# A cached attention block on one core: the last weight row as two partial loads, and rounds with branch hints moved

## The chip, the core and the metric

The kernel runs on one core of a Trainium2 chip, all in float32. The metric is the time of one execution in microseconds (us) on the device. A profiled execution gives the trace: when each instruction of TensorE (PE, with its weight loads as PEld), VectorE (DVE), ScalarE (ACT), GpSimd (POOL) and SyncE (SP) ran, and what the 16 DMA engines moved.

## The reference

One decoding step of two sequences: attention over a cache of 4096 positions with 32 heads of 128, beside a small feed-forward network, mixed by a gate.

```python
def reference(A_x, A_k_cache, A_v_cache, A_wq, A_wo, B_x, B_w1, B_w2, gate_w):
    x = A_x                                                  # (2, 1, 640)
    g = _sigmoid((x * gate_w).sum(-1, keepdims=True))
    q = (x @ wq).reshape(B, Sq, H, Dh) ...                   # B = 2, Sq = 1, H = 32, Dh = 128
    scores = jnp.einsum("bhqd,bhkd->bhqk", q, k_cache) * (Dh ** -0.5)
    p = _softmax(scores, axis=-1)
    o = jnp.einsum("bhqk,bhkd->bhqd", p, v_cache)
    a = o ... reshape(B, Sq, H * Dh) @ wo                    # wo: (4096, 640)
    b = silu(x @ w1) @ w2                                    # F = 1728
    return g * a + (1 - g) * b
```

The two caches hold 2 x 32 x 4096 x 128 floats each, 268 MB together; wq and wo have 10 MB each, w1 and w2 4.4 MB each.

## The kernel before, in words

`gated_decode` writes the whole program through a small recorder, `Flow`. `f.op` and `f.dma` note an operation with what it reads and writes; `f.plan` then works out which earlier operations each has to wait for, and the engine programs are put out one engine at a time. A DMA has a semaphore of its own and is waited for with a constant; `count` gives it a shared one. Line 72 of the profile is the DMA call in `Flow.dma`, lines 131, 153, 156, 172 and 176 are the waits and loop instructions.

Four ways of putting out operations matter here. `run` writes them straight. `repeat` writes one item's operations as a counted loop (PE's loop over the first 15 items). `climb` does so for DVE, two items a turn. `once` writes operations as the body of a loop that runs one time: a register is set to 0, the body begins with a place for a branch hint, and at the end 1 is added and a branch back to the head is tested and not taken.

```python
with nc.body(head, valid_engines=on):
    place = e.mark_branch_hint_location()
    self.run(eng, ops)
    nc.regs_alu(regs, regs, 1, op=ALU.add)
    e.br_lt(regs, 1, on_true=head, on_false=end).branch_hint(place)
```

Before the change one such round exists, on PE, around the last 33 operations (the whole output projection).

The stages. First w1, x, the gate's weights, w2 and wq are loaded (x and the gate's weights in rows of 640 bytes), DVE forms x @ w1 by multiply-adds (lines 474 and 477), PE the feed-forward output (line 569) into `ps_acc` and the queries (line 644). SP also writes zeros to the output at the start. Then come 16 items, an item being four heads of one sequence: its K is a slab of 128 partitions x 64 KiB, 8.39 MB, and so is its V. Three slabs of that size fill most of the on-chip memory: "v" for V, "a" and "b" for K of even and odd items. POOL (line 709) and DVE (line 715) multiply K by the query in place, DVE sums (line 725) and finds the maximum, ACT takes the exponentials (line 754), PE multiplies them by V in 32 groups (line 801), gathers (line 839), and DVE puts the heads' outputs into `oP` (lines 854 to 873). SP issues the K load of item i + 2 as soon as the sums of item i are done with that slab, and the V load of item i as soon as PE is done with V of item i - 1. The V of the last item goes to slab "a".

The output projection. The rows of wo form four groups of PR = 8 row sets; a row set is 128 partitions x 640 floats (2560 bytes a partition). `load_wo` issues, all behind the last V: groups 0 and 1 in one load of 5120 KB, group 2 in two loads of 1280 KB each (all into slab "v"), group 3 into slab "b" in three loads, of FIRST = 5 rows (1600 KB), 2 rows (640 KB) and the last row (320 KB). The keys `v.0` to `v.3` and `b.0` to `b.2` carry who waits for which load. `in_halves(g)` multiplies groups 0 to 2 with the heads in `oP` (line 592): each of 8 steps a group has two matmuls of 320 columns, to two blocks of 32 rows of `ps_acc`. In groups 0 and 1 the steps alternate between the upper and the lower 64 rows (`to = 64 * (s_ % 2)`); in group 2, from `PACED` on, all go to the upper 64. `merge` copies `ps_acc` to SBUF on ACT (line 604) and joins its parts into `ps_0` on PE (line 609). `in_quarters(3)` adds group 3 (line 622): 8 steps of four matmuls of 160 columns, the first five waiting for the first load, two for the second, one for the third. In the trace each matmul has two passes. DVE copies the result (line 930) and SP writes the output.

Of the kernel before, what the change touches and what calls it, by code (L numbers as in the profile page):

```python
# [189 lines left out]
def gated_decode(nc, x, kc, vc, wq, wo, w1, w2, gate, out):  # L190
    P = 128
    B, H, SK, DH = kc.shape
    D = x.shape[2]
# [13 lines left out]
    HB = 16  # L207
    CV = 68
    G = 4
    W = D // G  # L210
    W2 = D // 2
    NP = HQ // 2
    PR = 2 * Q
    FIRST = 5
    LEAD = HB // 2
    PACED = (NP - 2) * PR
    items = [(2 * n + u, b) for n in range(NP) for b in range(B) for u in range(2)]
    N = len(items)
    LOOPED = N - 1
# [2 lines left out]
    f = Flow(nc)  # L222
    V, S_, T_, G_ = nc.vector, nc.scalar, nc.tensor, nc.gpsimd

    def sb(name, shape, align=32):
        return nc.alloc_sbuf_tensor(name, shape, F32, align_bytes=align)[tuple([slice(None)] * len(shape))]

    def bank(name):
        return nc.alloc_psum_tensor(name, [P, 512], F32)[:, :]
# [4 lines left out]
    slab = {n: slabs[:, k * SLAB : (k + 1) * SLAB] for k, n in enumerate("vba")}  # L234

    def part(n, *ks):
        return [f"{n}.{k}" for k in (ks or range(8))]
# [13 lines left out]
    g = sb("g", [P, NP * B])  # L251
# [19 lines left out]
    oP, xs = oP_xs[:, : -D // Q], oP_xs[:, -D // Q :]  # L271
# [4 lines left out]
    ps_q, ps_o, ps_v, ps_acc, ps_t, ps_m, ps_0, ps_1 = (bank(f"ps{i}") for i in range(8))  # L276
    oT = ps_m[:64, 256:512].rearrange("p (n r) -> p n r", r=32)
    early, acc = ps_acc[:, :W2], ps_0[:, :W]

    h_e, h_v, h_o, *h_k = (f.sem(n) for n in ("weights", "values", "rows", "even", "odd"))  # L280


# [3 lines left out]
    PD = PR * D  # L286
# [15 lines left out]
    def load_k(i):  # L302
        n = kslab(i)
        f.dma("SP", slab[n], run_of(kflat, i), writes=part(n), count=(h_k[i % 2], 16 * (i // 2 + 1)))
# [10 lines left out]
    def load_wo(g):  # L315

        n, at = ("v", g * PD) if g < NP - 1 else ("b", 0)
        if g == 0:
            src = wo[: 2 * PR * P, :].rearrange("(g p n) d -> p g (n d)", g=2, n=PR)
            to = slab["v"][:, : 2 * PD].rearrange("p (g c) -> p g c", g=2)  # L320
            f.dma("SP", to, src, writes=part("v", 0, 1), after=v_users)
            return
        if g == 1:
            return
        src = wo[g * PR * P : (g + 1) * PR * P, :].rearrange("(p n) d -> p (n d)", n=PR)
        cuts = (0, PD // 2, PD) if g < NP - 1 else (0, FIRST * D, PD - D, PD)
        after = f.users(part(n)) if g == NP - 1 else v_users
        for k, (c0, c1) in enumerate(zip(cuts, cuts[1:])):
            f.dma("SP", slab[n][:, at + c0 : at + c1], src[:, c0:c1], writes=part(n, g % (NP - 1) + k), after=after)

# [8 lines left out]
        writes=part("v", 0),  # L341
# [7 lines left out]
            out=ident, in_=ident, compare_op=ALU.not_equal, fill=1.0, base=0, pattern=[[-1, P]], channel_multiplier=1  # L349
        ),  # L350
        reads=["ident"],
        writes=["ident"],
# [3 lines left out]
    f.op("POOL", lambda: G_.memset(seq, 0.0), writes=["seq"])  # L356

    out_rows = out.rearrange("b s (n d) -> (s n) b d", n=G)
    f.dma("SP", out_rows, oP[0:P:HB, :W], reads=["oP"], writes=["out"])

    f.op("DVE", lambda: V.memset(ones, 1.0), writes=["ones"])
    f.op(
# [2 lines left out]
        reads=["ident"],  # L365
        writes=["block"],
# [6 lines left out]
        reads=["block"],  # L373
        writes=["fold"],
# [4 lines left out]
        reads=["ident"],  # L379
        writes=["sel"],  # L380
# [4 lines left out]
        reads=["ident"],  # L385
        writes=["half"],
# [9 lines left out]
        reads=["sel"],  # L396
        writes=["pick"],
# [4 lines left out]
        reads=["sel"],  # L402
        writes=["own"],
# [4 lines left out]
        reads=["ident"],  # L408
        writes=["side"],
# [6 lines left out]
        reads=["block"],  # L416
        writes=["spread"],
# [4 lines left out]
        reads=["ident"],  # L422
        writes=["mask"],
    )
    f.op("DVE", lambda: V.memset(join, 0.0), writes=["join"])
    for e in range(2):
        ends, at = join[:, e, ::HB], 64 + HB * (1 - e)
# [5 lines left out]
            reads=["ident", "join"],  # L433
            writes=["join"],
        )
        for t in (at, at + 32):
# [3 lines left out]
                reads=["ident", "join"],  # L440
                writes=["join"],
# [10 lines left out]
        reads=["xs0", "xs1"],  # L452
        writes=["xt"],
# [5 lines left out]
        reads=["xt"],  # L459
        writes=["gx"],  # L460
    )
    f.op("DVE", lambda: V.reduce_sum(gp, gx.rearrange("p j b -> p b j"), axis=AX.X), reads=["gx"], writes=["gp"])
    rows = ps_v
# [4 lines left out]
    for b in range(B):  # L468
        for j in range(J):
            at = xt[:, j, HB * b : HB * b + 1]  # L470
# [11 lines left out]
                reads=part("a") + ["xt"],  # L482
                writes=[f"hsum{b}"],
            )

    def mm_hr():
# [18 lines left out]
        reads=["ones", "gp"],  # L505
        writes=["ps_o"],
# [6 lines left out]
        reads=["ge"],  # L513
        writes=["g"],
# [4 lines left out]
        reads=["g"],  # L519
        writes=["gc"],  # L520
# [7 lines left out]
    for e in range(2):  # L528
# [3 lines left out]
            reads=["ps_v"],  # L532
            writes=[f"spaced{e}"],
# [8 lines left out]
        reads=["he", "gc"],  # L542
        writes=["he"],
    )
    for e in range(2):
# [5 lines left out]
            reads=["he", "turned", "half", "seq"],  # L551
            writes=[f"seq{e}"],
# [27 lines left out]
    def heads(g):  # L580
        return [f"oP{g}{u}{b}" for u in range(2) for b in range(B)]

    def in_halves(g):

        for k in range(PR):
            s_ = g * PR + k

            def fn(k=k, s_=s_):
                to = 64 * (s_ % 2) if s_ < PACED else 0
                for n in range(2):  # L590
                    at = 32 * (k * NP + g) + LEAD // 2 * n
                    last = T_.matmul(  # L592
                        early[to + 32 * n : to + 32 * n + 32, :],
                        oP[:, at : at + 32],
                        slab["v"][:, s_ * D + n * W2 : s_ * D + (n + 1) * W2],
                        start=(s_ == 0),
                        stop=(s_ in (PACED - 1, PACED + PR - 1)),
                    )
                return last

            f.op("PE", fn, reads=part("v", g + (g == NP - 2 and k >= PR // 2)) + heads(g), writes=["ps_acc"])

    def merge():
        f.op("ACT", lambda: S_.copy(partial, early), reads=["ps_acc"], writes=["partial"])
# [73 lines left out]
    for u in range(2):  # L678
        for b in range(B):
# [7 lines left out]
                reads=[f"ps_{u}", "mask"],  # L687
                writes=[f"qall{u}{b}"],
# [9 lines left out]
    ops = {}  # L698
# [5 lines left out]
    def products(i):  # L704
        k = slab[kslab(i)].rearrange("p (c d) -> p c d", d=DH)
        k0, k1 = part(kslab(i), 0), part(kslab(i), 1)
        f.op(
            "POOL",
            lambda: G_.tensor_mul(k[:, CV:, :], k[:, CV:, :], qsb[:, None, :].to_broadcast([P, C - CV, DH])),  # L709
            reads=["qsb"] + k1,  # L710
            writes=k1,
        )
        f.op(
            "DVE",
            lambda: V.tensor_mul(k[:, :CV, :], k[:, :CV, :], ps_q[:, None, :DH].to_broadcast([P, CV, DH])),  # L715
            reads=["ps_q"] + k0,
            writes=k0,
        )
# [166 lines left out]

    steps = []
    for i in range(N + 1):
        j = i - 1  # L890
        loop = j if 0 <= j < LOOPED else None

        def by(what):
            return [ops[what, j]] if loop is not None else ()

        steps.append(len(f.ops["DVE"]))
        if i < N:
            products(i)
        if j >= 0:
            values(j, by=[v_load[j]] if loop is not None else (), loop=loop)  # L900
            invert(j)
        if 1 <= i < N:
            load_v(i)
        if i < N:
            scores(i)
            if i + 2 < N:
                load_k(i + 2)
            peak(i)
            weights(i)
        if i == N - 1:  # L910
            v_users = f.users(part("v"))
            for g_ in range(NP):
                load_wo(g_)
        if j >= 0:
            combine(j)
            gather(j, by=by("combine"), loop=loop)
            turn(j)
        if i < N:
            inner = i if i < LOOPED else None
            total(i, by=[ops["exp", i]] if i < LOOPED else (), loop=inner)  # L920
            if i + 1 < N:
                query(i + 1, by=[ops["exp", i]], loop=inner)
                copy_q(i + 1)
    edges = steps[2 : N + 1 : 2]
    f.alike["DVE"] = [[f.ops["DVE"][a:b] for a, b in zip(edges, edges[1:])]]
    for g_ in range(NP - 1):
        in_halves(g_)
# [20 lines left out]


    f.plan()  # L950
    for e in ("SP", "POOL", "ACT"):
        f.run(e)
    f.run("DVE", f.ops["DVE"][: edges[0]])
    f.climb("DVE", f.alike["DVE"][0])
    f.run("DVE", f.ops["DVE"][edges[-1] :])
    spans = {"PE": (len(f.ops["PE"]) - NP * PR - 1, len(f.ops["PE"]))}
    for e, (a, b) in spans.items():
        ops, at = f.ops[e], 0
        while at < len(ops):
            end = at  # L960
            if at == a:
                f.once(e, ops[a:b])
                at = b
            elif ops[at].loop is None:
                while end < len(ops) and ops[end].loop is None and end != a:
                    end += 1
                f.run(e, ops[at:end])
                at = end
            else:
                while end < len(ops) and ops[end].loop is not None:  # L970
                    end += 1
                f.repeat(e, ops[at:end], 1 + ops[end - 1].loop - ops[at].loop)
                at = end


_INS = ["A_x", "A_k_cache", "A_v_cache", "A_wq", "A_wo", "B_w1", "B_w2", "gate_w"]
# [18 lines left out]
```

## Time and profile before

| | |
|---|---|
| median of 3 runs | 696.22 us (695.77 to 696.24) |
| profiled execution | 696.45 us |
| its span, first to last instruction | 694.3 us |
| HBM read | 298.26 MB, 430 GB/s over the span |
| data queue's packets, share of 16 engines | 99.3% |
| busy: DVE, POOL, PE, ACT | 506.9, 265.6, 212.9, 40.0 us |
| instruction packets | 4: two on q8 (0.03 MB), two on q14 (0.02 MB) |

The span is what the trace shows; the execution's own time is about 2 us longer. A line of the profile's timeline gives the start and the duration in us, the engine, the line of the kernel, the operation with what it writes and reads, how many were merged, and in brackets how long the engine had been idle and what ended that. A line of the stretches gives for each engine its busy time and number of instructions, then the clock that was granted to TensorE (1.00 is full), the mean busy share of the 16 DMA engines and what they moved. A line of the queues gives packets, MB and the time they took as a share of 16 engines' time in that stretch.

### The profile page before, as it was taken

The numbers are of one execution on the slowest core, as the hardware profiler recorded it, in microseconds if no ns is written. First come the engines' busy times: TensorE is split into PE (matmuls) and PEld (weight loads), VectorE is DVE, ScalarE is ACT, GpSimd is POOL, SyncE is SP. The second block draws the span as 40 slices with busy tenths as digits, with TensorE's granted clock in tenths as the row PEclk, the third lists the DMA queues.
The fourth block names the chain that finished last, engine by engine and source line by source line (L and its number), as shares of the span: only waits on it lengthen the run. The fifth ranks groups of instructions, "written<-read, shape, count | busy, mean of one in ns | idle before, by whom it ended". The sixth has DMA issues, their size and how long they took to land. (4 is left out here: it accounts for less than half of the span.)

```text
span 694.3 us, 3766 instructions
## 1 busy us (share of the span) xinstructions
PE 212.9 (31%) x1440; PEld 70.8 (10%) x1440; DVE 506.9 (73%) x269; ACT 40.0 (6%) x152; POOL 265.6 (38%) x26
## 2 busy tenths in 40 slices
PE   0074032141331405060412306060503315060657
PEld 0032010010110101010100101010100101010113
DVE  3910958898989697886959596986959595977811
ACT  0001010101010101010010101010000101010000
POOL 1000908191827090815335180906244270907100
PEclk9988556575565757565665757575665757575689
DMA  9999999999999999999999999999999999999997
GB/s 381 431 438 462 427 423 428 423 464 430 427 430 423 453 438 431 427 427 427 461 430 427 430 423 461 434 427 430 423 457 434 430 427 427 427 461 430 427 416 317
DMA packets 6208, 298.32 MB, mean 430 GB/s; under 512 B 672, under 2 KB 700, under 8 KB 956
## 3 DMA queue, kind: packets, MB, share of 16 engines
q1 hardware_dynamic: 6204, 298.27, 99.3%
q8 instruction: 2, 0.03, 0.0%
q14 instruction: 2, 0.02, 0.0%
HBM read 298.26 MB, written 0.01 MB: 430 GB/s over the span
## 5 line engine op out<-in xcount | busy, mean ns | idle before, releaser
L709 POOL TENSOR_TENSOR slabs<-slabs,qsb 128x7680 f32<-128x7680 f32 x16 | 262.4, 16397 | 378.9 <-DMA slabs<-in_A_k_cache_dram 331.0
L725 DVE TENSOR_REDUCE s<-slabs 128x68 f32<-128x8704 f32 (+1 forms) x32 | 276.3, 8676 | 0.0
L801 PE MATMUL ps<-slabs,pz 128*32 128x512 f32 x1024 | 146.0, 734 | 337.6 <-PEq L156 330.7
L715 DVE TENSOR_TENSOR slabs<-slabs,ps 128x8704 f32<-128x8704 f32 x16 | 147.5, 9221 | 105.4 <-DMA slabs<-in_A_k_cache_dram 105.1
L801 PEld LDWEIGHTS ps<-slabs,pz 128*32 128x32 f32 x1024 | 39.7, 132 | 432.6 <-issue 425.7
L754 ACT ACTIVATE pz<-s,nb 32x128 f32<-32x128 f32 x64 | 25.5, 398 | 546.6 <-PE ps L801 390.3
L839 PE MATMUL ps<-osb,pick 128*128 128x512 f32 x32 | 20.4, 724 | 61.9 <-PEq L156 60.9
L823 DVE SCALAR_TENSOR_TENSOR osb<-ps,rg,own 128x512 f32<-128x512 f32 x16 | 12.0, 750 | 22.4 <-PE ps L801 22.3
L854 DVE TENSOR_REDUCE row<-ps 64x128 f32<-64x512 f32 x16 | 10.9, 682 | 23.3 <-PE ps L839 23.3
L775 PE MATMUL ps<-rs,fold 128*128 128x1 f32 x32 | 6.1, 260 | 40.0 <-PEq L156 39.9
L477 DVE SCALAR_TENSOR_TENSOR slabs<-slabs 128x1728 f32<-128x1728 f32 x8 | 16.1, 2018 | 0.3
L489 PE MATMUL ps<-slabs,xz_col 128*32 128x432 f32 x16 | 2.9, 887 | 33.3 <-DVE slabs L477 33.3
L839 PEld LDWEIGHTS ps<-osb,pick 128*128 128x128 f32 x32 | 5.4, 211 | 76.0 <-issue 74.1
L569 PE MATMUL ps<-slabs,seq 128*32 128x320 f32 x54 | 10.6, 559 | 3.7 <-DVE seq L548 3.7
L754 ACT ACTIVATION_READ_ACCUMULATOR pz<-s,nb 32x1 f32 x64 | 11.8, 184 | 0.0
L775 PEld LDWEIGHTS ps<-rs,fold 128*128 128x128 f32 x32 | 5.9, 219 | 53.1 <-issue 52.1
L861 DVE STREAM_TRANSPOSE ps<-row 64x256 f32<-64x256 f32 x16 | 10.3, 641 | 0.6
L644 PE MATMUL ps<-slabs,xz_col 128*32 128x512 f32 x80 | 9.8, 593 | 0.0
L592 PE MATMUL ps<-slabs,oP_xs 128*32 128x320 f32 x96 | 8.8, 434 | 1.3 <-DMA slabs<-in_A_wo_dram 1.3
L930 DVE COPY slabs<-ps 128x160 f32<-128x160 f32 x1 | 0.3, 325 | 12.1 <-PE ps L622 12.1
L654 PE MATMUL ps<-qall,spread 128*128 (+1 forms) x32 | 8.7, 360 | 0.8 <-ACT qall L682 0.8
L451 DVE STREAM_TRANSPOSE slabs<-oP_xs 128x160 f32<-128x160 f32 x1 | 0.5, 461 | 7.8 <-DMA oP_xs<-in_gate_w_dram 7.8
(63 smaller groups left out, 76.1 us busy)
## 6 DMA issues: line engine op xcount, KB each, us to landing
slabs<-in_A_wq_dram SPq DMA_DIRECT2D x1, 10240.0 KB, 44.6
slabs<-in_B_w_dram SPq DMA_DIRECT2D x2, 4320.0 KB, 17.1
slabs<-in_A_wo_dram SPq DMA_DIRECT2D x1, 5120.0 KB, 21.4
slabs<-in_A_wo_dram SPq DMA_DIRECT2D x2, 1280.0 KB, 25.3
slabs<-in_A_wo_dram SPq DMA_DIRECT2D x1, 1600.0 KB, 30.0
slabs<-in_A_wo_dram SPq DMA_DIRECT2D x1, 640.0 KB, 31.0
slabs<-in_A_wo_dram SPq DMA_DIRECT2D x1, 320.0 KB, 31.3
slabs<-in_A_k_cache_dram SPq DMA_DIRECT2D x16, 47.7
```

The lines of the kernel that those rows point to most:

```text
L477: lambda b=b, j=j, at=at: V.scalar_tensor_tensor(hsum[:, b, :], w1t[:, j, :], at, hsum[:, b, :], op0=ALU.mult, op1=ALU.add)
L569: last = T_.matmul(early[to : to + 32, :], seq[:, k : k + 2, :].rearrange("p k z -> p (k z)"), slab[n][:, k * HD : (k + 1) * HD], start=(k ...
L709: lambda: G_.tensor_mul(k[:, CV:, :], k[:, CV:, :], qsb[:, None, :].to_broadcast([P, C - CV, DH])),
L715: lambda: V.tensor_mul(k[:, :CV, :], k[:, :CV, :], ps_q[:, None, :DH].to_broadcast([P, CV, DH])),
L725: lambda c0=c0, c1=c1: V.reduce_sum(Ss[i % 2][:, c0:c1], k[:, c0:c1, :], axis=AX.X),
L754: last = S_.activation(pz[lo:hi, :, 4 * q : 4 * q + 4], s[lo:hi].rearrange("p (g c) -> p g c", c=4), AF.Exp, bias=nb[lo:hi], scale=SCALE, ...
L775: lambda *_: T_.matmul(ps_t[:, :1], fold.rearrange("p a q c -> p (a q c)"), rs, start=True, stop=True),
L801: last = T_.matmul(ps_v[32 * q : 32 * q + 32, :], pz[:, gr, :], v[:, gr, :], start=(gr < 4), stop=(gr >= NG - 4),)
L823: lambda: V.scalar_tensor_tensor(osb, ps_v.rearrange("p (c d) -> p c d", d=DH), rg, own[:, :, None].to_broadcast([P, 4, DH]), op0=ALU.mult ...
L839: lambda *_: T_.matmul(ps_o, pick, osb.rearrange("p c d -> p (c d)"), start=True, stop=True),
L854: lambda: V.reduce_sum(row, ps_o[:64].rearrange("p (c d) -> p d c", d=DH), axis=AX.X),
L861: lambda: V.transpose(oT.rearrange("p n (e i) -> p n e i", e=2), twice),
```

## The change

- The last row set of group 3 goes out as two loads, of the first `MOST = 6 * 12 = 72` partitions and of the other 56, which share a semaphore; PE waits for its full count, 32.
- Group 2 is loaded in one piece, and all its steps wait for that.
- In group 2 the steps alternate between the two 64-row parts of `ps_acc` as in the groups before; `PACED` is gone.
- The zeros that SP wrote to the output at the start are gone.
- PE's round around the output projection is gone; its operations are put out straight.
- ACT has a round around its operations of items 2 to 6, DVE one from its 31st operation (among the multiply-adds at line 477) to the start of its loop at item 2.

```diff
--- before.py
+++ after.py
@@ -213,7 +213,6 @@
     PR = 2 * Q
     FIRST = 5
     LEAD = HB // 2
-    PACED = (NP - 2) * PR
     items = [(2 * n + u, b) for n in range(NP) for b in range(B) for u in range(2)]
     N = len(items)
     LOOPED = N - 1
@@ -277,6 +276,7 @@
     oT = ps_m[:64, 256:512].rearrange("p (n r) -> p n r", r=32)
     early, acc = ps_acc[:, :W2], ps_0[:, :W]
 
+    MOST = 6 * 12
     h_e, h_v, h_o, *h_k = (f.sem(n) for n in ("weights", "values", "rows", "even", "odd"))
 
 
@@ -323,10 +323,16 @@
         if g == 1:
             return
         src = wo[g * PR * P : (g + 1) * PR * P, :].rearrange("(p n) d -> p (n d)", n=PR)
-        cuts = (0, PD // 2, PD) if g < NP - 1 else (0, FIRST * D, PD - D, PD)
+        cuts = (0, PD) if g < NP - 1 else (0, FIRST * D, PD - D, PD)
         after = f.users(part(n)) if g == NP - 1 else v_users
         for k, (c0, c1) in enumerate(zip(cuts, cuts[1:])):
-            f.dma("SP", slab[n][:, at + c0 : at + c1], src[:, c0:c1], writes=part(n, g % (NP - 1) + k), after=after)
+            to, rows = slab[n][:, at + c0 : at + c1], src[:, c0:c1]
+            if k < 2:
+                f.dma("SP", to, rows, writes=part(n, g % (NP - 1) + k), after=after)
+                continue
+            last = f.sem("last_row")
+            f.dma("SP", to[:MOST], rows[:MOST], after=after, count=(last, 16))
+            f.dma("SP", to[MOST:], rows[MOST:], writes=part(n, k), after=after, count=(last, 32))
 
 
 
@@ -356,7 +362,6 @@
     f.op("POOL", lambda: G_.memset(seq, 0.0), writes=["seq"])
 
     out_rows = out.rearrange("b s (n d) -> (s n) b d", n=G)
-    f.dma("SP", out_rows, oP[0:P:HB, :W], reads=["oP"], writes=["out"])
 
     f.op("DVE", lambda: V.memset(ones, 1.0), writes=["ones"])
     f.op(
@@ -586,7 +591,7 @@
             s_ = g * PR + k
 
             def fn(k=k, s_=s_):
-                to = 64 * (s_ % 2) if s_ < PACED else 0
+                to = 64 * (s_ % 2)
                 for n in range(2):
                     at = 32 * (k * NP + g) + LEAD // 2 * n
                     last = T_.matmul(
@@ -594,11 +599,11 @@
                         oP[:, at : at + 32],
                         slab["v"][:, s_ * D + n * W2 : s_ * D + (n + 1) * W2],
                         start=(s_ == 0),
-                        stop=(s_ in (PACED - 1, PACED + PR - 1)),
+                        stop=(s_ >= (NP - 1) * PR - 2),
                     )
                 return last
 
-            f.op("PE", fn, reads=part("v", g + (g == NP - 2 and k >= PR // 2)) + heads(g), writes=["ps_acc"])
+            f.op("PE", fn, reads=part("v", g) + heads(g), writes=["ps_acc"])
 
     def merge():
         f.op("ACT", lambda: S_.copy(partial, early), reads=["ps_acc"], writes=["partial"])
@@ -885,7 +890,7 @@
 
 
 
-    steps = []
+    steps, turns = [], []
     for i in range(N + 1):
         j = i - 1
         loop = j if 0 <= j < LOOPED else None
@@ -894,6 +899,7 @@
             return [ops[what, j]] if loop is not None else ()
 
         steps.append(len(f.ops["DVE"]))
+        turns.append(len(f.ops["ACT"]))
         if i < N:
             products(i)
         if j >= 0:
@@ -948,29 +954,24 @@
 
 
     f.plan()
-    for e in ("SP", "POOL", "ACT"):
+    for e in ("SP", "POOL"):
         f.run(e)
-    f.run("DVE", f.ops["DVE"][: edges[0]])
+    for e, a, b in (("ACT", turns[2], turns[7]), ("DVE", 30, edges[0])):
+        f.run(e, f.ops[e][:a])
+        f.once(e, f.ops[e][a:b])
+        f.run(e, f.ops[e][b:] if e == "ACT" else ())
     f.climb("DVE", f.alike["DVE"][0])
     f.run("DVE", f.ops["DVE"][edges[-1] :])
-    spans = {"PE": (len(f.ops["PE"]) - NP * PR - 1, len(f.ops["PE"]))}
-    for e, (a, b) in spans.items():
-        ops, at = f.ops[e], 0
-        while at < len(ops):
-            end = at
-            if at == a:
-                f.once(e, ops[a:b])
-                at = b
-            elif ops[at].loop is None:
-                while end < len(ops) and ops[end].loop is None and end != a:
-                    end += 1
-                f.run(e, ops[at:end])
-                at = end
-            else:
-                while end < len(ops) and ops[end].loop is not None:
-                    end += 1
-                f.repeat(e, ops[at:end], 1 + ops[end - 1].loop - ops[at].loop)
-                at = end
+    ops, at = f.ops["PE"], 0
+    while at < len(ops):
+        end = at
+        while end < len(ops) and (ops[end].loop is None) == (ops[at].loop is None):
+            end += 1
+        if ops[at].loop is None:
+            f.run("PE", ops[at:end])
+        else:
+            f.repeat("PE", ops[at:end], 1 + ops[end - 1].loop - ops[at].loop)
+        at = end
 
 
 _INS = ["A_x", "A_k_cache", "A_v_cache", "A_wq", "A_wo", "B_w1", "B_w2", "gate_w"]
```

## The prediction

> **What bounds the kernel now.** I read the page first: the slices, the queues, the chain that ended last.
>
> ```profile
> DMA  9999999999999999999999999999999999999997
> q1 hardware_dynamic: 6204, 298.27, 99.3%
> DMA 4%; PE 2%; SPq 0%; issue 0%; DVE 0%
> ```
>
> The 16 DMA engines are busy in every slice but the last. No engine's work sets the pace; bytes do. The change moves no bytes to speak of, so it can act only at the two ends: where the stream starts, and after it runs dry. The merged chain shows the second end.
>
> ```profile
> 659.47 29.95 DMA slabs<-in_A_wo_dram
> 689.42 0.14 issue
> 689.56 2.19 PE ps L622 x56
> 691.75 0.01 issue
> 691.75 0.51 PE ps L622 x8
> ```
>
> From the landing of the fourth group's first five rows (689.42) the chain is 2.19 us of matmuls that partly wait for the next two rows and for the last one, then 0.51 us for the last row, the copy, and the output. Stretches of the last microseconds, with the DMA engines' share in the last column but one, show how the stream runs dry:
>
> ```profile
> core 0: us, PE busy (x) PEld busy (x) DVE busy (x) ACT busy (x) POOL busy (x), PEclk, DMA share, GB/s
> 689.50:690.00 0.50, 0.44 (x16) 0.46 (x20) 0.00 (x0) 0.00 (x0) 0.00 (x0) 1.00 0.94 379
> 690.00:690.30 0.30, 0.30 (x19) 0.29 (x12) 0.00 (x0) 0.00 (x0) 0.00 (x0) 1.00 0.41 162
> 690.30:690.60 0.30, 0.30 (x16) 0.29 (x12) 0.00 (x0) 0.00 (x0) 0.00 (x0) 1.00 0.24 94
> 690.60:691.00 0.40, 0.40 (x16) 0.17 (x8) 0.00 (x0) 0.00 (x0) 0.00 (x0) 1.00 0.16 64
> 691.00:691.40 0.40, 0.40 (x16) 0.35 (x16) 0.00 (x0) 0.00 (x0) 0.00 (x0) 1.00 0.11 45
> ```
>
> The engines don't finish together. A share of 0.11 is 1.8 engines of 16: two still run at 691.0 to 691.4, when most were done by 690.3. What is left after 690.0 is 0.3 x 0.41 + 0.3 x 0.24 + 0.4 x 0.16 + 0.4 x 0.11 = 0.30 us per engine, so an even finish would come near 690.3, 1.1 us sooner. Who made two engines late? The queues of three short stretches (54 to 56, 109 to 113, 276 to 278 us) show instruction blocks on the same engines:
>
> ```profile
> q8 instruction: 1, 0.02, 3.0%
> ...
> q8 instruction: 1, 0.02, 1.5%
> q14 instruction: 1, 0.01, 0.5%
> ...
> q14 instruction: 1, 0.01, 1.0%
> ```
>
> 3.0% of 16 engines in 2 us is 0.96 us on one engine; 1.5% in 4 us is again 0.96; the q14 packets are 0.32 us each. Since the data queue never empties, an engine that fetched a block stays behind to the end. Two engines late by about 1 us and two by a third: this is the shape of the tail above. Which engines these are, no view tells.
>
> **The change part by part.** First the tail's compute.
>
> ```profile
> 679.53 4.18 PEld L592 LDWEIGHTS ps<-slabs,oP_xs 128*32 128x32 f32 x66 [2.10 <-DMA slabs<-in_A_wo_dram]
> 685.75 0.12 PEld L592 LDWEIGHTS ps<-slabs,oP_xs 128*32 128x32 f32 x2 [0.15 <-DMA slabs<-in_A_wo_dram]
> 687.63 0.12 PEld L592 LDWEIGHTS ps<-slabs,oP_xs 128*32 128x32 f32 x2 [0.15 <-issue]
> 688.39 0.42 ACT L604 COPY slabs<-ps 128x320 f32<-128x320 f32 x1 [28.27 <-PE ps L592]
> 688.87 0.47 PE L609 MATMUL ps<-slabs,join 128*17 128x160 f32 x8 [0.53 <-ACT slabs L604]
> 689.53 1.25 PEld L622 LDWEIGHTS ps<-slabs,oP_xs 128*17 128x17 f32 x40 [0.53 <-issue]
> 691.01 0.41 PEld L622 LDWEIGHTS ps<-slabs,oP_xs 128*17 128x17 f32 x16 [0.23 <-DMA slabs<-in_A_wo_dram]
> 691.75 0.13 PEld L622 LDWEIGHTS ps<-slabs,oP_xs 128*17 128x17 f32 x8 [0.34 <-DMA slabs<-in_A_wo_dram]
> 692.64 0.58 SPq L72 DMA_DIRECT2D out_dram<-slabs  x1
> ```
>
> The last row as 72 and 56 partitions. Before, the two-row load releases PE at 691.01 and the last row, 128 partitions of 2560 bytes, at 691.75: a late engine needs 0.74 us for its eighth, 0.093 us a partition. The diff writes 72 as 6 x 12; if the 56 go as 4 x 14, twelve engines carry ten partitions, two carry four, two none. Best case: the late two carry none, the last row is in by 691.01, and PE has 24 weight loads left instead of 8: 0.41 + 0.13 = 0.54, then 0.51 - 0.13 = 0.38 until the last matmul ends, so 691.93 against 691.75 + 0.51 = 692.26. Gain 0.33 us. Worst case: the late ones are among the twelve, and two partitions more cost 2 x 0.093 = 0.19. I take -0.33: the split's shape (two engines with nothing, two with half) is that of the lateness in the rows, two by 0.96 and two by 0.32; the ends stay -0.33 and +0.19. SP issues one load more here and one less in the third group: six as before.
>
> [...]
>
> Third group in one load, no pacing. PE now waits for all of it, that is till 685.75, where the second half releases it now. Its 32 matmuls then run over two row pairs alternately as the first two groups do: 66 loads in 4.18 us, 0.063 each, so 32 take 2.0. ACT's copy starts now 0.64 us after the last two weight loads (687.63 + 0.12 = 687.75); the same again gives 685.75 + 2.0 + 0.64 = 688.39, the very time of now. The join still ends at 688.87 + 0.47 = 689.34, just ahead of the five rows that land at 689.42: 0. Its cover is only 0.08 us: should the five rows land sooner, the join is what PE waits for next.
>
> Rounds with hints. PE loses one round, ACT and DVE get one each: a register move, a hint, an add and a branch. DVE's starts in the first stage's last multiplies and ends before the third item, ACT's spans items 2 to 6. Behind them wait SP's issues of K and V. The cover:
>
> ```profile
> 33.32 0.34 SPq L72 DMA_DIRECT2D slabs<-in_A_k_cache_dram  x1
> 50.60 8.94 PE L644 MATMUL ps<-slabs,xz_col 128*32 128x512 f32 x75
> 68.67 9.22 DVE L715 TENSOR_TENSOR slabs<-slabs,ps 128x8704 f32<-128x8704 f32 x1 [28.41 <-DMA slabs<-in_A_k_cache_dram]
> ...
> slabs<-in_A_k_cache_dram SPq DMA_DIRECT2D x16, 47.7
> slabs<-in_A_v_cache_dram SPq DMA_DIRECT2D x16, 29.4
> ```
>
> A load of K or V is 8.39 MB, 19.5 us at the page's 430 GB/s. [...] What the hints do to the four fetches the trace of before can't show. Bounds: all four vanish, or one more of 0.96 us comes at the end. I take 0 and keep both as rivals.
>
> No early zeros.
>
> ```profile
> 4.18 0.59 SPq L72 DMA_DIRECT2D out_dram<-oP_xs  x1
> ```
>
> SP loses 0.59 us at 4.18 and next issues at 33.32: 0; 5 KB leave the stream: 0.01. The last output becomes the kernel's first write to its tensor. Its issue took 0.59 early and 0.58 late, so being first costs the issue nothing. For the landing, bounds: 0, and another 694.3 - 692.64 - 0.58 = 1.1 us. I take 0.
>
> **Sum.** -0.33 + 0 + 0 + 0 on the profiled 696.45 is 696.12. That execution stands 0.23 above the median of 696.22; against the median it is 695.9.
>
> **The rivals.**
> All fetches leave the stream or the tail evens out wholly. Everything lands near 690.3, the five rows 1.1 us before 689.42. Then the join at 689.34 is the start: 689.34 + 1.25 + 0.54 + 0.38 gives 691.51, 0.75 sooner than 692.26: 695.5. For it: DVE's and ACT's rounds lie over the fetches at 109 to 113 and 276 us. Against it: the one at 54 us, 0.96, falls where only PE computes.
>
> The split misses the late engines. +0.19, so 696.4. For it: nothing in the profile numbers the engines.
>
> PE without its round fetches in the tail (the slower side). q8 is likely PE's: at 54 us PE alone computes (L644 above; DVE idles 28.41 us before 68.67). Its round held all matmuls of the tail, and from 650 to 694 us the only queue is that of the data:
>
> ```profile
> q1 hardware_dynamic: 1118, 16.91, 89.6%
> ```
>
> If the round's hint kept a block away and it now comes after 658, one engine falls 0.96 us behind for good. An ordinary engine then ends at 690.3 + 0.19 + 0.96 = 691.45, and 691.45 + 0.51 = 691.96 is still no loss against 692.26. It decides from the point where it hits one of the late two, whose two rows then come at 691.97: 691.97 + 0.54 + 0.38 = 692.89, +0.63: 696.9. If PE itself stands for its code, add the packet's 0.96 once more, less the join's slack of 0.08: 697.8.
> [...]
>
> PE's clock falls in the new pause. With the pacing gone PE idles from about 683.8 to 685.75, where this trace has it busy throughout (the last row here).
>
> ```profile
> 667.40:670.80 3.40, 3.38 (x16) 0.80 (x20) 0.00 (x0) 0.00 (x0) 0.00 (x0) 0.50 0.95 410
> 676.00:679.50 3.50, 1.31 (x6) 0.30 (x2) 1.92 (x3) 0.00 (x0) 0.00 (x0) 1.00 0.99 424
> 683.80:685.60 1.80, 1.80 (x18) 0.82 (x14) 0.00 (x0) 0.00 (x0) 0.00 (x0) 1.00 1.00 427
> ```
>
> After the wait for the last V, from 660.5 to 667.4, the granted clock was 0.50 for 3.4 us. At half rate the third group takes 4.0 instead of 2.0, the join ends at about 691.34 instead of 689.34, and 691.34 + 1.25 + 0.54 + 0.38 = 693.51, +1.25: 697.5. Against it: from 676.0 to 679.5 PE was busy for 1.31 of 3.50 us, idle for longer than the new pause, and the clock stayed at 1.00.
>
> **How the numbers follow.** The likeliest, 695.9, has 0.45 (its own range 695.5 to 696.2). Split missed, 696.4: 0.25. PE's fetch, 696.9 to 697.8: 0.12. Clock, 697.5: 0.07. All even, 695.5: 0.10. The first write dear, up to +1.1 - 0.33, 697.0: 0.01. The range runs from 695.1, which is 695.5 less the 0.45 by which one of the three runs shown stood under their median, to 697.3; what it leaves out is the clock's case and PE's stand. A measurement can tell 0.2%, 1.4 us, so faster means under 694.8 and slower over 697.6: no case reaches the first, and only PE's stand or two cases together the second. 0.03, 0.92, 0.05.
>
> **What would show it.** Right: the share after 690.6 is nearly nil, PE's last 24 weight loads run in one piece from about 691.0, the copy at L930 starts near 692.0. The split missed: the last 8 loads wait for a DMA till 691.9. PE's fetch: an instruction packet after 650 us. The clock: 0.50 in a stretch after 684. The pacing's end: L592 pauses near 684 and its copy starts at about 688.4 all the same. Wrong altogether if the stream's rate or its start moved: a gap in the DMA slices, or the first K load landing later than 68.6.

## The result and the profile after

The changed kernel takes 696.91 us (median of 22 runs, 696.74 to 697.69) against 695.95 us before (695.60 to 696.87): 0.96 us slower, a ratio of 1.0014 with a 95% interval of 1.0008 to 1.0020. The forecast was 695.9, a third of a microsecond faster; the sign was wrong, and the loss lies inside the 0.2% that I had called the smallest that counts.

The profiled execution after has a span of 695.7 us instead of 694.3. Its chain of waits, start and duration in us:

```profile
658.80 33.72 DMA slabs<-in_A_wo_dram
692.52 0.04 issue
692.56 1.05 PE ps L627 x24
693.62 0.02 issue
693.64 0.32 DVE slabs L936
```

The chain used to hang on the first five rows of the fourth group (landed 689.42) with the rest dribbling in. Now it hangs on the two-row load, which lands at 692.52. In the trace before it released PE at 691.01. PE then runs its last 24 weight loads in one piece, as forecast, only 1.5 us later. The stretches of the end, in the columns of the prediction's:

```profile
689.50:690.00 0.50, 0.00 (x0) 0.00 (x0) 0.00 (x0) 0.00 (x0) 0.00 (x0) 1.00 0.98 251
690.00:690.30 0.30, 0.10 (x4) 0.13 (x8) 0.00 (x0) 0.00 (x0) 0.00 (x0) 1.00 0.87 222
690.30:690.60 0.30, 0.30 (x12) 0.29 (x14) 0.00 (x0) 0.00 (x0) 0.00 (x0) 1.00 0.58 137
690.60:691.00 0.40, 0.40 (x20) 0.39 (x13) 0.00 (x0) 0.00 (x0) 0.00 (x0) 1.00 0.39 83
```

Read the last two columns together. Before, 0.94 of the engines moved 379 GB/s, and 0.41 moved 162: about 400 GB/s for a full share. Now 0.98 move 251, 0.87 move 222, 0.58 move 137 and 0.39 move 83: 213 to 256. The engines are busy and get less done. The single packets in the trace say the same: in the kernel before every packet of 2560 bytes after 689 us takes 0.10 us, in the changed kernel those that start from 690.3 to 691.0 take 0.13 to 0.21. That is no lateness; something slows them all.

A second thing is new. The queues from 684 to 686 us, and below them those from 100 to 684 us:

```profile
q1 hardware_dynamic: 70, 0.84, 100.1%
q8 instruction: 1, 0.02, 3.0%
...
q1 hardware_dynamic: 4640, 253.29, 100.1%
q8 instruction: 1, 0.02, 0.0%
```

A 0.02 MB block of instructions now comes in the tail, at 684.95, 3.0% of 16 engines in 2 us, again 0.96 us on one engine: the very rival I had named for the slower side. And the two q14 packets that before had between 100 and 300 us are gone. So two stories compete for the same 1 us: theory R, the lost round of PE and its late block; theory S, the split of the last row.

### The profile page after: what moved, and what is told of

It is laid out like the page before. It is cut to its first block, busy times and chain, and to the rows that moved or that the text cites. A ratio compares the mean times of both kernels' runs of the same rounds, so it can differ in the third digit from the quotient of the medians.

```text
span 695.7 us, 3768 instructions
## 1 busy us (share of the span) xinstructions
PE 209.6 (30%) x1440; PEld 69.6 (10%) x1440; DVE 506.9 (73%) x269; ACT 40.0 (6%) x152; POOL 265.6 (38%) x26
## 5 line engine op out<-in xcount | busy, mean ns | idle before, releaser
L936 DVE COPY slabs<-ps 128x160 f32<-128x160 f32 x1 | 0.3, 324 | 12.4 <-PE ps L627 12.4
L597 PE MATMUL ps<-slabs,oP_xs 128*32 128x320 f32 x96 | 6.9, 434 | 2.2 <-DMA slabs<-in_A_wo_dram 2.2
## 6 DMA issues: line engine op xcount, KB each, us to landing
slabs<-in_A_k_cache_dram SPq DMA_DIRECT2D x16, 47.7
slabs<-in_A_v_cache_dram SPq DMA_DIRECT2D x16, 29.4
```

## The experiments

**Which part.** Four kernels, each compared with the kernel before on the same chip.

PE's round put back into the changed kernel:

```diff
+    spans = {"PE": (len(f.ops["PE"]) - NP * PR - 1, len(f.ops["PE"]))}
...
+            if at == a:
+                f.once(e, ops[a:b])
```

> The changed kernel with PE's round around the output projection put back; all else as changed. Theory R (the lost round lets a 16 KiB block of PE's code be fetched at 685 us, and the engine that carries it is late to the end): no instruction packet between 600 and 694 us, the two-row load lands near 691.2 instead of 692.5, time about 1.2 us under the changed kernel, that is 0.2 to 0.3 us under the kernel before. Theory S (the last row's two partial loads slow the late engines): the packet may go, but the two-row load still lands after 692.0, and at least 0.7 us of the loss against before stays.

The last row whole again in the changed kernel:

```diff
-            f.dma("SP", to[:MOST], rows[:MOST], after=after, count=(last, 16))
-            f.dma("SP", to[MOST:], rows[MOST:], writes=part(n, k), after=after, count=(last, 32))
+            f.dma("SP", to, rows, writes=part(n, g % (NP - 1) + k), after=after)
```

> The changed kernel with the last row in one load of 128 partitions; PE still without its round. Theory R: the packet at 685 us stays and with it most of the loss, 0.7 to 1.0 us above before. Theory S: the share of the DMA engines after 690.0 falls as before, GB/s per share is near 390 instead of 235, and the time is within 0.3 us of before.

PE's round taken from the kernel before (the first diff, reversed):

> The kernel before with PE's round taken away, nothing else. Theory R: an instruction packet of 0.02 MB on q8 at about 684 us, and 0.6 to 1.0 us more than before. Theory S: with or without a packet, within 0.3 us of before.

The kernel before with the split alone (the second diff, reversed):

> The kernel before with its last row as loads of 72 and 56 partitions, nothing else. Theory R, with my prediction's term: 0.33 us faster (late engines relieved) to 0.19 us slower (late ones among the twelve). Theory S: the two-row load lands about 1 us later than 691.0, GB/s per share of the DMA engines after 690 falls from 390 to near 235, and the time is 0.6 to 1.0 us above before.

| kernel | median us | before, same chip | ratio (95%) |
|---|---|---|---|
| changed, PE's round back | 696.57 | 695.87 | 1.0008 (0.9999 to 1.0017) |
| changed, last row whole | 696.02 | 695.87 | 1.0001 (0.9992 to 1.0010) |
| before, no PE round | 695.89 | 695.87 | 0.9999 (0.9990 to 1.0008) |
| before, split | 696.88 | 695.87 | 1.0012 (1.0003 to 1.0021) |

The split alone makes the loss, 1.0 us on the kernel before; without it the changed kernel is where before is. Theory R falls as the cause, though its mechanism exists. The queues of the kernel before without PE's round, from 684 to 686 us, and its last stretches:

```profile
q8 instruction: 1, 0.02, 3.0%
```

```profile
690.60:691.00 0.40, 0.40 (x20) 0.39 (x13) 0.00 (x0) 0.00 (x0) 0.00 (x0) 1.00 0.26 102
691.00:691.40 0.40, 0.40 (x20) 0.20 (x12) 0.00 (x0) 0.00 (x0) 0.00 (x0) 1.00 0.19 77
```

The block comes, and 0.19 of the engines instead of 0.11 are still at work after 691: one engine more. In this trace the last row releases PE at 692.08 instead of 691.75, 0.33 us later, but the times show no loss (695.89 against 695.87): the branch "an ordinary engine, still no loss" of the rival. With PE's round back in the changed kernel the block is gone and 0.7 us of loss stay. That interval just reaches 1, but in the trace the two-row load still releases PE only at 692.14. The 0.3 us that the round took off is within the intervals, so a small price of the block beside the split is neither shown nor excluded.

The split alone on the kernel before, and the changed kernel with a whole row, in the same stretches:

```profile
690.30:690.60 0.30, 0.30 (x16) 0.29 (x12) 0.00 (x0) 0.00 (x0) 0.00 (x0) 1.00 0.77 171
690.60:691.00 0.40, 0.40 (x20) 0.39 (x15) 0.00 (x0) 0.00 (x0) 0.00 (x0) 1.00 0.75 186
```

```profile
689.50:690.00 0.50, 0.35 (x12) 0.37 (x16) 0.00 (x0) 0.00 (x0) 0.00 (x0) 1.00 0.78 312
690.00:690.30 0.30, 0.30 (x16) 0.29 (x12) 0.00 (x0) 0.00 (x0) 0.00 (x0) 1.00 0.28 111
```

171 / 0.77 = 222 and 186 / 0.75 = 248 GB/s for a full share with the split, 312 / 0.78 = 400 without. The slow rate goes with the split.

**What in the split.** Four theories: it is uneven (U); one more small load costs by itself (N); any load of half of the partitions is slow (H); or it matters into which partitions the engines write at one time (P). Two cuts of the last row, and two of the third group, where the effect would be large. For P I put at most 0.2 us for columns and 0.5 to 1.2 us for halves of 64; for the third group 3 to 6 us and about 215 GB/s in block halves, at most 0.5 us as even and odd.

```diff
+            f.dma("SP", to[:, : D // 2], rows[:, : D // 2], after=after, count=(last, 16))
+            f.dma("SP", to[:, D // 2 :], rows[:, D // 2 :], writes=part(n, k), after=after, count=(last, 32))
```

> The kernel before with its last row as two loads again, but cut by columns: each has all 128 partitions, with half of each partition's 2560 bytes. [...] Theory N (numbers: one more small load, or smaller packets, cost by themselves): the loss of the 72 and 56 split, 0.7 to 1.0 us, comes back.

```diff
+            f.dma("SP", to[:64], rows[:64], after=after, count=(last, 16))
+            f.dma("SP", to[64:], rows[64:], writes=part(n, k), after=after, count=(last, 32))
```

> The kernel before with its last row as loads of 64 and 64 partitions. All 16 engines can have equal parts of each, so nothing is uneven. Theory P: 0.5 to 1.2 us above before, GB/s per share after 690 us near 200 to 250. Theory U (uneven: twelve engines carry ten partitions instead of eight): within 0.2 us of before. Theory N: 0.7 to 1.0 us above before.

```diff
+            if g == 2:
...
+                    f.dma("SP", to[:64], rows[:64], after=after, count=(half, 16))
+                    f.dma("SP", to[64:], rows[64:], writes=part(n, 2, 3), after=after, count=(half, 32))
```

> The kernel before with its third group loaded as partitions 0 to 63 and 64 to 127, 1280 KB each, in place of two loads of half the columns, 1280 KB each. Same bytes, same number of loads, even over 16 engines. [...] Theories N and U: within 0.3 us of before.

The same with `to[0:P:2]` and `to[1:P:2]`:

> As the kernel whose third group goes as partitions 0 to 63 and 64 to 127, but with the even and then the odd partitions. [...] Theory H (any load with half of the partitions is slow, or its many single rows are): as slow as the halves in blocks.

| kernel | median us | before, same chip | ratio (95%) |
|---|---|---|---|
| last row by columns | 696.17 | 695.76 | 1.0004 (0.9995 to 1.0013) |
| last row 64 and 64 | 697.09 | 695.76 | 1.0017 (1.0008 to 1.0026) |
| third group in block halves | 708.19 | 695.76 | 1.0173 (1.0157 to 1.0188) |
| third group even and odd | 696.86 | 695.76 | 1.0017 (1.0008 to 1.0027) |

The halves of 64, which 16 engines can share evenly, cost 1.3 us (P had 0.5 to 1.2), more than 72 and 56: U falls. By columns the time is 0.4 us above before, more than the 0.2 of theory P, and the interval (up to 0.9 us) does not by itself exclude N's 0.7. The traces do. The halves of 64 first, the columns below:

```profile
690.00:690.30 0.30, 0.30 (x16) 0.29 (x12) 0.00 (x0) 0.00 (x0) 0.00 (x0) 1.00 0.88 196
690.30:690.60 0.30, 0.30 (x17) 0.29 (x11) 0.00 (x0) 0.00 (x0) 0.00 (x0) 1.00 0.77 145
```

```profile
690.00:690.30 0.30, 0.30 (x20) 0.29 (x12) 0.00 (x0) 0.00 (x0) 0.00 (x0) 1.00 0.59 218
690.30:690.60 0.30, 0.30 (x19) 0.29 (x12) 0.00 (x0) 0.00 (x0) 0.00 (x0) 1.00 0.24 90
```

For a full share these are 223 and 188 GB/s with the halves, 369 and 375 with the columns. The two-row load releases PE at 692.10 with the halves; with the columns it does at 691.03 and the last row at 691.82, against 691.01 and 691.75 before. So one more small load costs next to nothing: N falls.

The third group in block halves costs 12.4 us. Its stretches, and those of the kernel before below them:

```profile
678.00:681.00 3.00, 0.25 (x1) 0.00 (x0) 1.76 (x4) 0.00 (x0) 0.00 (x0) 0.99 1.00 191
681.00:684.00 3.00, 2.35 (x20) 0.99 (x24) 0.00 (x0) 0.00 (x0) 0.00 (x0) 0.50 1.03 212
684.00:688.00 4.00, 3.47 (x51) 1.21 (x40) 0.00 (x0) 0.00 (x0) 0.00 (x0) 0.96 1.11 236
688.00:692.00 4.00, 0.00 (x0) 0.00 (x0) 0.00 (x0) 0.00 (x0) 0.00 (x0) 0.90 1.01 190
```

```profile
678.00:681.00 3.00, 1.73 (x25) 0.77 (x28) 1.77 (x4) 0.00 (x0) 0.00 (x0) 1.00 0.98 416
681.00:684.00 3.00, 3.00 (x50) 1.45 (x44) 0.00 (x0) 0.00 (x0) 0.00 (x0) 1.00 1.05 445
```

All 16 engines are fully busy and move 190 to 236 GB/s in place of 416 to 445: half. That is the rate of theory P, but P had only 3 to 6 us for it. PE's instructions in that kernel show where the 12.4 us arise:

```profile
681.65 5.81 PE L599 MATMUL ps<-slabs,oP_xs 128*32 128x320 f32 x64 [3.40 <-DMA slabs<-in_A_wo_dram]
695.31 5.80 PE L599 MATMUL ps<-slabs,oP_xs 128*32 128x320 f32 x32 [7.85 <-DMA slabs<-in_A_wo_dram]
701.64 0.47 PE L616 MATMUL ps<-slabs,join 128*17 128x160 f32 x8 [0.53 <-ACT slabs L611]
```

The third group's second half lands at 695.3 instead of 685.75. These 9.6 us alone are more than P allowed. The slow stretch begins while the load before it is still under way (PE gets groups 0 and 1 at 681.65 instead of 679.53), and it lasts beyond 692: from 692 to 696 a share of 0.83 moves 269 GB/s, 324 for a full share, which no run here explains. The other 2.5 us are PE: from that landing to the issue of the output it takes 704.70 - 695.31 = 9.4 us instead of 692.64 - 685.75 = 6.9. All 32 matmuls of the group come after the landing, paced (all to the same 64 rows), and at first at half the clock (0.50 granted from 692 to 696, 0.75 in the mean from 696 to 700) after 7.85 us of idling; they take 5.8 us. The join and the fourth group follow them.

Even and odd, the same bytes in as many loads, bring the stream back, so H falls. Its last stretch and its end beside it:

```profile
688.00:692.00 4.00, 3.47 (x60) 1.94 (x60) 0.00 (x0) 0.43 (x1) 0.00 (x0) 1.00 0.56 228
```

```profile
690.06 0.43 ACT L611 COPY slabs<-ps 128x320 f32<-128x320 f32 x1 [30.43 <-PE ps L599]
690.54 0.13 PEld L616 LDWEIGHTS ps<-slabs,join 128*17 128x17 f32 x8 [1.11 <-ACT slabs L611]
690.69 2.15 PEld L629 LDWEIGHTS ps<-slabs,oP_xs 128*17 128x17 f32 x64
```

A share of 0.56 at 228 GB/s is 407, as ever. Its 1.1 us, more than the 0.5 that P allowed, has another source: PE has to wait for both halves and then runs the paced group, so ACT's copy starts at 690.06 instead of 688.39, and the 64 weight loads come after everything has landed. It is the price of one load for the third group *with* the pacing left in; the change takes the pacing out.

**What is left of the change, and two checks.**

```diff
-    for e in ("SP", "POOL", "ACT"):
...
+    for e, a, b in (("ACT", turns[2], turns[7]), ("DVE", 30, edges[0])):
+        f.run(e, f.ops[e][:a])
+        f.once(e, f.ops[e][a:b])
```

The kernel before with these rounds alone:

> The kernel before with the rounds on ACT and DVE added, nothing else. If the rounds keep the two 8 KB blocks of q14 away: no q14 packet between 100 and 300 us, two late engines instead of four after 690 us, but the last landing, set by the two that carried 16 KB blocks, stays: within 0.2 us of before. If the rounds cost time on the way (a stall for code that reaches SP's issues): more than 0.3 us above.

It took 695.89 us against 695.82 (0.9999, 0.9990 to 1.0008). The rounds do keep the q14 blocks away. The queues from 100 to 300 us are below, first of this kernel, then of the kernel before:

```profile
q8 instruction: 1, 0.02, 0.0%
```

```profile
q8 instruction: 1, 0.02, 0.0%
q14 instruction: 2, 0.02, 0.0%
```

The tail shows it too. From 690.3 to 690.6 us the share was 0.24, now it is 0.11, about two engines of 16 instead of four:

```profile
690.30:690.60 0.30, 0.30 (x20) 0.29 (x12) 0.00 (x0) 0.00 (x0) 0.00 (x0) 1.00 0.11 43
```

But from 691.0 to 691.4 the share is still 0.08 (0.11 before), and the last row releases PE at 691.65 instead of 691.75: the engines that set the end are others, so it buys nothing.

The changed kernel with both suspects undone (PE's round back, last row whole):

> The changed kernel without the two parts under suspicion: the last row whole and PE's round back. What is left of the change is the rounds on ACT and DVE, the third group in one load without pacing, and no early zeros. With theory P and the late engines unmoved by the rest: two late engines set the last landing as before, 0.3 us under before to 0.1 above. A rival (the remaining parts cost something that the split hid): more than 0.3 us above before.

696.08 us against 695.82 (1.0001, 0.9992 to 1.0011): a little more than the 0.1 us above that was expected, and less than the rival's 0.3. Nothing else in the change moves the time by an amount that can be told.

The last row as even and odd partitions, `to[0:P:2]` and `to[1:P:2]`:

> The kernel before with its last row as even and odd partitions, 64 each. [...] Theory N (a second load of single short rows costs by itself): 0.7 to 1.3 us above before.

696.03 us against 695.84 (1.0004, 0.9995 to 1.0013), within the 0.3 us that I put for P. Its rows run at 162 / 0.41 = 395 and 77 / 0.20 = 385 GB/s for a full share:

```profile
690.00:690.30 0.30, 0.30 (x16) 0.29 (x12) 0.00 (x0) 0.00 (x0) 0.00 (x0) 1.00 0.41 162
690.30:690.60 0.30, 0.30 (x17) 0.29 (x11) 0.00 (x0) 0.00 (x0) 0.00 (x0) 1.00 0.20 77
```

Its two-row load releases PE at 690.95 and its last row at 691.69. Theory P holds at the last row too: even and odd or in blocks, the loads have the same size and number (in the third group also the same 6080 packets in the whole execution), and only the blocks are slow.

What this shows is that the choice of partitions decides. Through what it does is not shown. A cut by partitions also changes which rows of `wo` the engines read, and no run changes one without the other.

**Which engines are late.** Loads of few partitions as probes:

```diff
+            for m in (2, 4, 8, 12, 14):
+                f.dma("SP", slab["b"][:m, PD + m * P : PD + (m + 1) * P], wo[:m, :P], writes=[f"probe{m}"], ...)
```

> The changed kernel with the last row whole and PE's round back; behind the last row SP issues five probe loads of 2, 4, 8, 12 and 14 partitions (512 bytes each, to unused columns), and the output waits for them too. If such loads go on that many lowest-numbered engines, a probe lands late as soon as it includes an engine that is late. Theory T (the late two are among the last four engines, as the split needs): the probes of 2 to 12 partitions land near 690.4, only that of 14 or none near 691.7. Theory F (they are among the first twelve): a probe of at most 12 partitions lands near 691.7, and so would part of the 72 partitions have done.

This one told nothing: the probes waited for the last row and SP issued them only at 691.84, when all queues were empty. (It took 698.06 us; the probes came ahead of the output.) With the probes queued directly behind the last row:

> The changed kernel with the last row whole and PE's round back, and, queued right behind the last row, probe loads of 2, 4, 8, 12 and 14 partitions (512 bytes each, to unused columns). GpSimd fills one column after each, in this order, so the start of each fill is the landing of its probe; the output waits for the fills. Theory T (the late two are the last ones, numbers 14 and 15, as the split needs): all five fills start near 690.6 to 691.0. Theory F (they are among the first twelve): from one of the first four probes on, the fills start near 691.7 or later, and the split could not have relieved them.

```profile
690.39 0.69 POOL L919 MEMSET mark<- 128x1 f32 x4 [45.29 <-DMA slabs<-in_A_wo_dram]
691.80 0.10 POOL L919 MEMSET mark<- 128x1 f32 x1 [0.72 <-DMA slabs<-in_A_wo_dram]
```

The first four fills (2, 4, 8 and 12 partitions) ran from 690.39 to 691.08, the fifth waited till 691.80. That the fifth probe was the last in the queue is not the reason: the trace records the landing of every engine's part, and of the 14 parts of this probe twelve landed by 691.13 and two at 691.65 and 691.75, while all 12 parts of the probe before it landed by 690.94. So in this one execution the two late engines are among those of the probe of 14 and not among those of the probe of 12: neither theory had it. Counted from 0, with each probe taken to add engines to those of the one before, they are numbers 12 and 13. If the 72 partitions went on the same twelve engines as the probe of 12 and the 56 on the same 14 as the probe of 14, the split gave these two four partitions instead of eight: half of the relief I had counted. The trace of the changed kernel fits: the engine that finishes last writes its last two-row packet till 691.97 and then four packets of 2560 bytes.

Hence a last trial: 108 and 20 partitions, if they go as 9 x 12 and 2 x 10, would leave them nothing.

```diff
-    MOST = 6 * 12
+    MOST = 9 * 12
```

> The changed kernel with PE's round back and the last row as 108 and 20 partitions instead of 72 and 56. The probes put the two late engines at numbers 12 and 13; if 108 goes as 9 x 12 and 20 as 2 x 10, these carry nothing of the last row. [...] Theory Q (any block of part of the partitions costs about the same): 0.6 us or more above before, like the 72 and 56 with PE's round (0.7).

696.59 us against 695.79 (1.0011, 1.0002 to 1.0020). For P I had put 0.2 us above at most and the two-row load within 0.3 us of 691.0. That missed: 0.8 us slower, which is what theory Q gave (0.6 or more).

```profile
690.00:690.30 0.30, 0.30 (x17) 0.29 (x12) 0.00 (x0) 0.00 (x0) 0.00 (x0) 1.00 0.70 231
690.30:690.60 0.30, 0.30 (x19) 0.29 (x11) 0.00 (x0) 0.00 (x0) 0.00 (x0) 1.00 0.34 77
...
691.76 0.40 PEld L627 LDWEIGHTS ps<-slabs,oP_xs 128*17 128x17 f32 x16 [1.06 <-DMA slabs<-in_A_wo_dram]
```

The rate holds up better, 330 and 226 GB/s for a full share, yet the two-row load still comes 0.75 us late (691.76 against 691.01). From 690.6 to 691.0 a share of 0.11 moves 19 GB/s, 173 for a full share, and in the trace its last two-row packets take 0.33 to 0.37 us each instead of 0.20. What slows them, when by the probes the late engines carry nothing of the last row, no run shows.

## Why the prediction was right or wrong

The step that failed is the term "the last row as 72 and 56 partitions". I bounded it by -0.33 and +0.19 and took -0.33; alone on the kernel before it measured +1.0 us. Both ends counted only the bytes that each engine *carries*, at 0.093 us a partition. That price came from a load of all 128 partitions whose engines ran at their full rate, and I kept it for loads of part of the partitions. Neither end asked which partitions the engines work on at one time. The runs showed that blocks slow the engines, those still at work on the two-row load too: 222 GB/s for a full share instead of 400, and a two-row load that comes 1.5 us later. No row of the trace before shows a partial load of size, so the bound above was too narrow. The relief, too, was by the probes only half of what I counted. "The split misses the late engines" had the right sign and a fifth of the size.

The measured 696.91 is also the figure of another rival, PE's fetch (696.9), and its block did come. That is a coincidence: with the block and a whole last row the changed kernel took 696.02, and the kernel before with the split and without the block 696.88.

That 72 partitions go on twelve engines and 56 on fourteen, from which the -0.33 was counted, was my assumption; no row of the trace before shows it. The landings in the traces fit it: 12 and 14 for the probes of 12 and 14 partitions, 26 for the 72 and 56 (12 + 14), 22 for the 108 and 20 (12 + 10). Which engines these are, no run shows, and none shows the gain of 0.33 us: in its place the split alone measured +1.0 us.

The other steps. *Fetches*: the profile's shares did name them rightly as what makes engines late, and the rounds on ACT and DVE do suppress two of them; I took 0 for the time, and 0 it was (695.89 against 695.82 us with the rounds alone). How long an engine waits for a block of its instructions, no run shows; the cover that the trace before shows is a landing of K and V 47.7 and 29.4 us after the issue (medians), for loads of 19.5 us. *PE's round*: its removal brings the block at 684.95, as the rival said, onto one engine, without a loss that can be told (696.02 and 695.89 us with the block, against 695.87). *Third group in one load, no pacing*: forecast 0, with a pause near 684 and ACT's copy still at 688.4; in the changed kernel:

```profile
686.00 2.36 PE L597 MATMUL ps<-slabs,oP_xs 128*32 128x320 f32 x32 [1.52 <-DMA slabs<-in_A_wo_dram]
688.42 0.42 ACT L609 COPY slabs<-ps 128x320 f32<-128x320 f32 x1 [28.97 <-PE ps L597]
...
693.99 0.60 SPq L72 DMA_DIRECT2D out_dram<-slabs  x1
```

*Clock*: 1.00 granted in all stretches from 683.8 on, so the pause of 1.5 us did not lower it. *No early zeros*: from the output's issue to the span's end 695.7 - 693.99 = 1.7 us, before 694.3 - 692.64 = 1.7: 0, as taken.

That the whole would stay under 0.2% was right, but the certainty about its parts was misplaced: of the five steps the only one I gave a gain to was the only one with a price that can be told.

## What to carry to other kernels

Divide the GB/s of a stretch by the busy share of the DMA engines. Here a low share at the full rate (0.41 at 162 GB/s) was a queue running dry, and a full share at half the rate (1.01 at 190) was engines that were busy and moved half as much. Where a load of all 128 partitions has to be cut, try columns, or even and odd partitions: in this kernel's last row both cost nothing that could be told (0.4 and 0.2 us, within the intervals), while every cut into blocks of partitions, even of the last 320 KB, cost 0.7 us or more. When a bound is taken from rows that all have one shape, its upper end doesn't cover an operation of another shape.

## What the runs showed of the hardware

An instruction block of 0.02 MB took one DMA engine 0.96 us, one of 0.01 MB 0.32 us, and the delay was still there at the end of the stream (its queue was busy for 99.3% of 16 engines' span): without the two q14 blocks (0.01 MB each) of 113 and 277 us the share from 690.3 to 690.6 us was 0.11 instead of 0.24, some 400 us after the second. One-time loops with a branch hint kept such blocks out of the stream: on ACT and DVE the two q14 packets between 100 and 300 us, on PE the one at 685 us (none from 600 to 694 us with the round back). Whether the loop or its hint does it, no run separates. Two loads in blocks of 64 partitions about halved the rate of the 16 engines in the third group, to 190 GB/s at the lowest, while the profile showed them busy (shares of 1.00 to 1.11); loads of the even and the odd partitions left it at 411 to 437 GB/s from 678 to 688 us.
